# A gated S5 layer on one Trainium2 core: earlier norms and statistics, B in four transposes, and tanh gates until the phase tables are done

## The chip, the core and the metric

The kernel runs on one core of a Trainium2 chip. The metric is device time in microseconds (us) of one execution; the profile of an execution shows a span that is about 1.8 us shorter than its time. Executions are told apart by the mean clock that TensorE was granted: the kernel before has executions near 220.5 us at a clock of 0.975 and executions near 225.3 us at 0.953. The record calls an execution slow when it is over 1.5% above the fastest of its kernel in the call, and ratios use fast executions alone.

The engines are TensorE (PE, matmuls), VectorE (DVE), ScalarE (ACT) and GpSimd (POOL).

## The reference, cut to what matters

The input is 2048 tokens of width 448 in bfloat16. A layer norm feeds two branches, whose product is added to the input:

```python
def reference(A_x, ...):
    x = A_x
    xn = _layernorm(x)                       # mean and variance over the 448 columns
    # branch A, S5: a complex diagonal recurrence over the tokens
    #   Bu = xn @ B_bar ; h[t] = Lam_bar * h[t-1] + Bu[t] ; y = 2*Re(h @ C) + xn*Dskip
    s = _A_ref(xn, ...)
    # branch B: (sigmoid(xn @ w_gate) * (xn @ w_up)) @ w_down, inner width 1792
    g = _silu(_B_ref(xn, ...))
    return x + s * g
```

## The kernel before

The tokens go in 4 chunks of 512 (4 tiles of 128 tokens each). For each chunk TensorE computes 14 gate units (`gu`: a gate and an up product, 1.62 us a unit), 4 B units (`bu`), 4 down products (2.65 us each) and 4 y products (1.51 us each). ScalarE takes the gate and B results out of PSUM, the memory that matmuls write to (an eviction); VectorE multiplies, runs the scan and finishes y. A plan, made when the program is built, lays the engines' instructions in order: `side` is a queue of VectorE work put between matmul units, `add_late` defers work until a planned time, `force` plays the queues forward until a condition holds.

The row statistics are per chunk. Two VectorE instructions a tile give mean and variance; a chain of about 20 operations on 128x4 elements then makes the row scale `rsd` (a reciprocal square root, by three Newton steps for every chunk but chunk 0). In the kernel before, chunk 0's chain is on VectorE, the others' on GpSimd:

```python
def stat_chain(g, t0, n):
    G = V if g == 0 else nc.gpsimd
    ...                                        # cut: cast, + eps, negated mean
    for _ in range(3):
        G.tensor_tensor(out=q, in0=y, in1=y, op=ALU.mult)
        G.tensor_tensor(out=q, in0=q, in1=ve, op=ALU.mult)
        G.tensor_scalar(out=q, in0=q, scalar1=-0.5, scalar2=1.5, op0=ALU.mult, op1=ALU.add)
        G.tensor_tensor(out=y, in0=q, in1=y, op=ALU.mult)
    G.tensor_tensor(out=sd_b, in0=y, in1=ve, op=ALU.mult)

    def fin():
        V.reciprocal(out=rsd[:, ts, :], in_=sd_b)
        rs_done.add(g)
    plan.add_late(plan.dve + T_CHAIN, 0.15, fin)
```

The statistics come late, and the norms stand at fixed places, whether their chain is done or not (`force` puts the reciprocal in front):

```python
for pt in range(4):
    side += [... nu_1 .. nu_4 of pt ...]       # cut: sine and cosine tables of the recurrence
side.append((0.0, emit_edges))
side.append((0.9, emit_neg))
side.append((2.2, emit_coeffs))
for i in range(4):
    side.append((0.7, lambda i=i: stat(2, 8, i, 4)))
side.append((0.0, lambda: stat_chain(2, 8, 4)))
...                                            # chunk 3's statistics: inside the scan of chunk 0

def norm_slot(tt, on_vector):
    ...                                        # cut
    xm = norm_a(tt, False)                     # ScalarE
    plan.force(lambda: tt // CT in rs_done)
    norm_b(tt, xm, False)                      # ScalarE, needs rsd
    dup(tt)                                    # GpSimd copy of 64 columns
    dma_transpose(tt)                          # xn -> xnT, which feeds the matmuls
...
run_phase(G(0, 2, 8) + mixed(G(0, 8, 14), Bs(0), 2), [], spread(norms(1, True), 4, 5) + [(3, b_fix)])
run_phase(u, spread(downs(0), 1, 8), spread(norms(2), 2, 8))
run_phase(u, spread(ys(0), 2, 4) + spread(downs(1), 3, 8), spread(norms(3), 1, 7))
```

B arrives in 8 transposing transfers, and one GpSimd copy (`b_fix`, into `bT`) moves a part to its place; in GpSimd's order it stands behind chunk 1's chain. The first 16 gate units use tanh and the others use sigmoid; tanh is in the same ScalarE table as the sine here (in the traces no table load stands between them), so that tables are loaded 4 times in all.

Of the kernel before, what the change touches and what calls it, by code (L numbers as in the profile page):

```python
# [36 lines left out]
N_TANH = FT + 2  # L37
# [72 lines left out]
def kernel(  # L110
# [26 lines left out]
    plan = Plan()  # L137

# [5 lines left out]
    warm = w.tile([P, 512], BF16, name="warm")  # L144
    nc.gpsimd.memset(warm[:], 0.0)
# [16 lines left out]
    bT = w.tile([P, 4, 7 * P], BF16, name="bT")  # L162
    bw = w.tile([P, 1, 384], BF16, name="bw")
# [3 lines left out]
    vrow = w.tile([1, 3, 512], BF16, name="vrow")  # L167
# [11 lines left out]
    def load_b():  # L179
        for k, mat in enumerate((A_B_re, A_B_im)):  # L180
            a, b = 384 * k, 768 + H * k
            nc.sync.dma_start_transpose(out=bT[:, 0:3, a:a + 384], in_=mat[0:384, 0:384])
            if k == 0:
                nc.sync.dma_start_transpose(out=bw[:], in_=mat[0:384, 320:448])
            else:
                nc.sync.dma_start_transpose(out=bT[:, 3:4, a:a + 384], in_=mat[0:384, 320:448])
            nc.sync.dma_start_transpose(out=bT[:, 0:3, b:b + H], in_=mat[384:448, 0:384])
            nc.sync.dma_start_transpose(out=bT[:, 3:4, b:b + H], in_=mat[384:448, 320:448])
# [12 lines left out]
    load_w(512, 1152)  # L201
    load_b()
    load_w(1152, F)
# [3 lines left out]
    load_x(8, 4)  # L207
    load_x(12, 4)
# [3 lines left out]
    def emit_warm(n):  # L212
        for _ in range(n):
            nc.tensor.matmul(wps[:, 0, :], lhsT=warm[:, 0:P], rhs=warm[:], start=True, stop=True)  # L214
# [4 lines left out]
    T_CHAIN = 9.0  # L219
# [11 lines left out]
    def stat_chain(g, t0, n):  # L231

        G = V if g == 0 else nc.gpsimd
        mv = mvs[g]

        def t(name, dt=FP32):
            return w.tile([P, n, 1], dt, name=f"{name}{g}")[:]

        ts = slice(t0, t0 + n)
        var_b, ve_b, mean_b = t("var_b", BF16), t("ve_b", BF16), t("mean_b", BF16)  # L240
        G.tensor_copy(out=var_b, in_=mv[:, :, 1:2])
        G.tensor_single_scalar(out=ve_b, in_=var_b, scalar=EPS, op=ALU.add)
        if g == 0:
            sd_b = t("sd_b", BF16)
            nc.scalar.activation(sd_b, ve_b, ACT.Sqrt)
        G.tensor_copy(out=mean_b, in_=mv[:, :, 0:1])
        G.tensor_single_scalar(out=nmean[:, ts, :], in_=mean_b, scalar=-1.0, op=ALU.mult)
        if g == 0:
            V.reciprocal(out=rsd[:, ts, :], in_=sd_b)
            return  # L250
        ve, y, q, sd_b = t("ve"), t("y"), t("q"), t("sd_b", BF16)
        G.tensor_copy(out=ve, in_=ve_b)
        G.tensor_scalar(out=y.bitcast(I32), in0=ve.bitcast(I32), scalar1=-0.5, scalar2=RS_MAGIC,
                        op0=ALU.mult, op1=ALU.add)
# [8 lines that stand above are left out]
            V.reciprocal(out=rsd[:, ts, :], in_=sd_b)  # L263
            rs_done.add(g)

        plan.add_late(plan.dve + T_CHAIN, 0.15, fin)

# [27 lines left out]
    def pe_transpose(tt, eng):  # L295
        xn, xnT, j = xns[tt // CT][:, tt % CT, :], xnTs[tt // CT], tt % CT
        tp = ps.tile([P, 4, P], BF16, name="tpx", tag="acc", bufs=2)
        for kt in range(4):
            nc.tensor.transpose(tp[:, kt, :], xn[:, kt * P:(kt + 1) * P], ident[:, :])
        dst = xnT[:, :, j * P:(j + 1) * P]  # L300
# [36 lines left out]
    ones = cp.tile([P, NTAB], BF16, name="ones", tag="xnd_", bufs=1)  # L337

# [5 lines left out]
    def emit_columns():  # L344
# [9 lines left out]
        nc.scalar.activation(dt_b[:], vps[:, 0, :], ACT.Exp)  # L354
        K.update(vps=vps, vsb=vsb, dt_b=dt_b, lre=vsb[:, 1, :], lim=vsb[:, 2, :])

    def emit_decay():
        V.tensor_copy(out=K["vsb"][:], in_=K["vps"][:])
# [79 lines left out]
    def c_steps():  # L438
        cT = w.tile([P, 7, D], BF16, name="cT")
        K["cT"] = cT  # L440
        steps = []

        def step(dst, r, re, im, sa, sb):
            tmp = fp.tile([P, D], FP32, name="ctmp", tag="sig")
            nc.scalar.activation(tmp[r, :], re, ACT.Copy, scale=sa)
            V.scalar_tensor_tensor(out=dst, in0=im, scalar=sb, in1=tmp[r, :], op0=ALU.mult, op1=ALU.add)

        for m in range(7):
            def go(m=m):
                c2, n2i, n2r = K["c2"], K["n2i"], K["n2r"]  # L450
                if m < 6:
                    pt = m % 3
                    sa, sb = (c2, n2i) if m < 3 else (n2i, n2r)
                    step(cT[:, m, :], slice(0, P), crT[:, pt, :], ciT[:, pt, :], sa[:, pt:pt + 1], sb[:, pt:pt + 1])
                else:
                    hi = slice(H, P)
                    step(cT[0:H, 6, :], hi, cw[hi, 0, :], cw[hi, 1, :], c2[hi, 3:4], n2i[hi, 3:4])
                    step(cT[hi, 6, :], hi, cw[hi, 0, :], cw[hi, 1, :], n2i[hi, 3:4], n2r[hi, 3:4])
            steps.append((0.65 if m < 6 else 1.3, go))
        return steps  # L460
# [25 lines left out]
    LO, HI, ALL = slice(0, H), slice(H, P), slice(0, L)  # L486
    hFs = {}
    hF_done = set()
    n_gate = [0]
# [17 lines left out]
    def gu_act(c, ft):  # L507
# [3 lines left out]
        tanh = n_gate[0] < N_TANH  # L511
        n_gate[0] += 1
# [24 lines left out]

    def bu_unit(c, pt, half_first):
        bu = ps.tile([P, 2, 512], FP32, name="bu")
        if pt < 3:  # L540
            ms, halves = (pt, pt + 3), ((LO, bT[LO, 3, pt * P:(pt + 1) * P]), (HI, bT[HI, 3, 384 + pt * P:384 + (pt + 1) * P]))
        else:
            ms, halves = (6,), ((HI, bT[HI, 3, 768:896]),)
        unit_mms([bu[:, i, :] for i in range(len(ms))], ALL, xnTs[c],
                 [(lambda kt, m=m: bT[:, kt, m * P:(m + 1) * P]) for m in ms], halves, half_first)
# [110 lines left out]
    T_UNIT, T_ACT, T_DOWN, T_Y = 1.55, 1.3, 2.65, 1.55  # L656
# [38 lines left out]
    act(scr[:], pio2[:], ACT.Exp)  # L695
# [6 lines left out]
    for i in range(2):  # L702
        stat(0, 0, i, 4)
    emit_decay()
    for i in range(2, 4):
        stat(0, 0, i, 4)
    act(scr[:], pio2[:], ACT.Sqrt)
    stat_chain(0, 0, 4)
    nc.gpsimd.memset(ones[:], 1.0)
    for j in range(2):  # L710
        norm_b(j, norm_a(j, True), True)
        dup(j)
        pe_transpose(j, "v")
        emit_warm(1)
    xm = [norm_a(j, False) for j in (2, 3)]
    for j in (2, 3):
        norm_b(j, xm[j - 2], False)
        dup(j)
    act(scr[:], pio2[:], ACT.Silu)
    A, B = slice(0, 256), slice(256, 512)  # L720
    for f in range(2):
        gu_mm(0, f, A, f == 1)
    for j in (2, 3):
        pe_transpose(j, "v")
    for f in range(2):
        gu_mm(0, f, B, f == 1)
    plan.pe = plan.dve = 0.0
    for f in range(2):
        cost, fin = gu_act(0, f)
        plan.add_late(1.2 + 1.1 * f, cost, fin)  # L730

    side = plan.side
    side.append((0.6, emit_theta))
    side.append((1.2, emit_iota))
    new_xn(1)
    new_xnT(1)
    for i in range(4):
        side.append((0.7, lambda i=i: stat(1, 4, i, 4)))
    side.append((0.0, lambda: stat_chain(1, 4, 4)))
# [3 lines left out]
    side.append((0.0, emit_edges))  # L743
    side.append((0.9, emit_neg))
    side.append((2.2, emit_coeffs))
    for i in range(4):
        side.append((0.7, lambda i=i: stat(2, 8, i, 4)))
    side.append((0.0, lambda: stat_chain(2, 8, 4)))

    def ssm(c):  # L750
        side.append((1.15, lambda: emit_xnd(c)))
        ss = ssm_steps(c)
        if c == 0:
            st3 = [(0.7, lambda i=i: stat(3, 12, i, 4)) for i in range(4)]
            st3.append((0.0, lambda: stat_chain(3, 12, 4)))
            extra = c_steps() + st3
# [10 lines left out]
    def norm_slot(tt, on_vector):  # L767
        if tt % CT == 0 and tt >= 8:
            new_xn(tt // CT)
            new_xnT(tt // CT)  # L770
        if on_vector:
            V_norm(tt)
            return
        xm = norm_a(tt, False)
        plan.force(lambda: tt // CT in rs_done)
# [4 lines left out]
    def V_norm(tt):  # L780
        def fin():
            plan.force(lambda: tt // CT in rs_done)
            norm_b(tt, norm_a(tt, True), True)
            dup(tt)
            dma_transpose(tt)
            xn_done.add(tt)
        plan.add_late(plan.pe, 0.8, fin)

    def run_phase(units, sides, extras):

        n = len(units) // 2
        for p in range(n):
# [5 lines left out]
            for q, fn in extras:  # L798
                if q == p:
                    fn()  # L800
# [26 lines left out]
    def norms(c, a=False):  # L827
        return [lambda i=i: norm_slot(c * CT + i, a) for i in range(CT)]

    def b_fix():  # L830
        nc.gpsimd.tensor_copy(out=bT[LO, 3, 0:384], in_=bw[HI, 0, :])

    run_phase(G(0, 2, 8) + mixed(G(0, 8, 14), Bs(0), 2), [], spread(norms(1, True), 4, 5) + [(3, b_fix)])
# [4 lines left out]
    run_phase(u, spread(downs(0), 1, 8), spread(norms(2), 2, 8))  # L838
    ssm(2)
    u = mixed(G(2, 0, 4), Bs(2)) + G(2, 4, 14)  # L840
    run_phase(u, spread(ys(0), 2, 4) + spread(downs(1), 3, 8), spread(norms(3), 1, 7))
# [34 lines left out]
```

## Time and profile before

| | before (first profile) |
|---|---|
| time, median of 3 | 224.98 us (220.81 to 225.73) |
| profiled execution | 225.65 us, span 223.9, clock 0.953: a slow one |
| TensorE busy | 199.6 us |
| VectorE busy | 178.2 us |
| ScalarE busy | 121.5 us |
| GpSimd busy | 33.4 us |

The page of the profile, its busy times, its rows for TensorE and TensorE's clock in 40 equal slices (tenths, 9 is full), and the shares of the chain that ended last:

```profile
span 223.9 us, 2849 instructions
...
PE 199.6 (89%) x978; PEld 83.6 (37%) x978; DVE 178.2 (80%) x379; ACT 121.5 (54%) x218; POOL 33.4 (15%) x88
...
PE   7689985989998399938999999999999999969993
...
PEclk9969996799999889995999999999999999999999
...
DVE 51%; PE 22%; POOL 12%; ACT 8%; issue 4%; DMA 1%; POOLq 0%; ACTq 0%
```

TensorE is the busiest, and it has three holes: slices 7, 14 and 18 (a slice is 5.6 us). Near each the clock row falls too. TensorE's timeline shows them. Its columns are start, length, engine, line, operation, out<-in, sizes and count; in brackets is the idle time before it, and what ended it:

```profile
36.31 0.60 PE L476 MATMUL bu<-xnT,bT 64*128 64x512 bf16 x2 [3.58 <-POOL bT L831]
...
37.27 1.46 PE L470 MATMUL gu<-xnT,wg 128*128 128x512 bf16 x3
...
76.23 0.39 PE L476 MATMUL bu<-xnT,bT 64*128 64x512 bf16 x2 [4.29 <-ACT bus_857 L548]
76.56 2.74 PE L470 MATMUL bu<-xnT,bT 128*128 128x512 bf16 x6
...
101.71 1.46 PE L470 MATMUL gu<-xnT,wg 128*128 128x512 bf16 x3 [4.42 <-DMA xnT<-xn]
```

Each idle ends with a different releaser. After the first and the third, three matmuls of a gate take 1.46 us, where elsewhere in the same trace three take 0.81 us: half the clock, 0.43 us a matmul instead of 0.216. After the second, six matmuls of B take 2.74 us, where six took 1.46 at 31.27 us. The Trainium skill, "TensorE: Matmul & The Clock Gate", section "What's actually happening", says that the clock falls to half after one idle window of about 3.4 us; these three idles, of 3.58 to 4.42 us, agree with it.

What lies behind them shows on GpSimd and ScalarE. GpSimd's timeline, the first and the last operation of chunk 1's chain, and the copy behind it:

```profile
26.17 0.68 POOL L241 CAST var_b_418<-mv_362 128x4 bf16<-128x4 f32 x1 [15.04 <-DVE mv_362 L226]
...
35.49 0.20 POOL L260 TENSOR_TENSOR sd_b_428<-y_426,ve_425 128x4 bf16<-128x4 f32 x1
35.75 0.50 POOL L831 COPY bT<-bw 64x384 bf16<-64x384 bf16 x1
```

ScalarE's timeline, before the second hole:

```profile
73.64 0.67 ACT L289 ACTIVATE xn<-xm,rsd 128x448 bf16<-128x448 bf16 x1 [5.36 <-DVE rsd L263]
...
75.16 1.02 ACT L548 CAST bus_857<-bu 128x1024 bf16<-128x1024 f32 x1
```

GpSimd's timeline, before the third hole, the copy for the last tile of chunk 2:

```profile
98.99 0.23 POOL L293 COPY xn<-xn 128x64 bf16<-128x64 bf16 x1
```

The chain on GpSimd took 9.5 us, and the copy of B that TensorE needs came only after it. For chunk 2 a norm on ScalarE waited 5.36 us for the row scale, and the eviction that TensorE needs stood behind that norm. The copy at 98.99 us stood behind chunk 3's chain, which was on GpSimd until 99.04, and the transpose of the third hole came after the copy.

### The profile page before, as it was taken

The numbers are of one execution on the slowest core, as the hardware profiler recorded it, in microseconds if no ns is written. First come the engines' busy times: TensorE is split into PE (matmuls) and PEld (weight loads), VectorE is DVE, ScalarE is ACT, GpSimd is POOL, SyncE is SP. The second block draws the span as 40 slices with busy tenths as digits, with TensorE's granted clock in tenths as the row PEclk, the third lists the DMA queues.
The fourth block names the chain that finished last, engine by engine and source line by source line (L and its number), as shares of the span: only waits on it lengthen the run. The fifth ranks groups of instructions, "written<-read, shape, count | busy, mean of one in ns | idle before, by whom it ended". The sixth has DMA issues, their size and how long they took to land.

```text
span 223.9 us, 2849 instructions
## 1 busy us (share of the span) xinstructions
PE 199.6 (89%) x978; PEld 83.6 (37%) x978; DVE 178.2 (80%) x379; ACT 121.5 (54%) x218; POOL 33.4 (15%) x88
## 2 busy tenths in 40 slices
PE   7689985989998399938999999999999999969993
PEld 2254331323433133412344444434434444425551
DVE  5736993481998179996669999999999999999943
ACT  2816673578782898731574657656443555501310
POOL 5100284010068101860000000000000000000000
PEclk9969996799999889995999999999999999999999
DMA  5995799230000111000032010100000000001001
GB/s 125 297 211 85 237 313 214 81 74 3 0 1 0 23 26 23 0 11 14 0 26 65 21 44 1 26 0 0 21 22 23 21 0 0 3 21 63 0 21 62
DMA packets 23268, 12.19 MB, mean 54 GB/s; under 512 B 14643, under 2 KB 23222, under 8 KB 23254
## 3 DMA queue, kind: packets, MB, share of 16 engines
q1 hardware_dynamic: 23200, 11.90, 21.5%
q0 software_dynamic: 48, 0.11, 0.6%
q8 instruction: 7, 0.11, 0.2%
q14 instruction: 7, 0.06, 0.1%
q10 hardware_dynamic: 6, 0.00, 0.0%
HBM read 6.77 MB, written 1.84 MB: 38 GB/s over the span
## 4 chain that ended last, share of the span: by engine, by line
DVE 51%; PE 22%; POOL 12%; ACT 8%; issue 4%; DMA 1%; POOLq 0%; ACTq 0%
DVE wv L584 9%; PE gu L470 8%; PE acc L665 5%; DVE stats L225 3%; DVE hT L604 3%; PE acc L680 3%; DVE g_t L686 3%; DVE tb L565 2%; DVE ta L565 2%; DVE hFa L526 2%; DVE z L578 2%; DVE hFb L526 2%; PE bu L470 2%; DVE x_all L687 2%; PE wps L214 2%
## 5 line engine op out<-in xcount | busy, mean ns | idle before, releaser
L470 PE MATMUL gu<-xnT,wg 128*128 128x512 bf16 (+1 forms) x174 | 48.9, 393 | 6.0 <-DMA xnT<-xn 4.4
L470 PE MATMUL gu<-xnT,wu 128*128 128x512 bf16 (+1 forms) x174 | 48.5, 390 | 0.0
L519 ACT ACTIVATE sig<-gu 128x512 bf16<-128x512 f32 x40 | 23.9, 597 | 30.2 <-PE gu L476 22.8
L470 PEld LDWEIGHTS <-wg 128*128 128x128 bf16 x174 | 15.6, 101 | 31.3 <-issue 14.6
L470 PEld LDWEIGHTS <-wu 128*128 128x128 bf16 x174 | 17.8, 102 | 21.1 <-issue 2.8
L668 ACT ACTIVATE sigd<-acc 128x448 bf16<-128x448 f32 x16 | 8.7, 541 | 30.3 <-PE acc L665 30.3
L665 PE MATMUL acc<-wd,hFb 128*128 128x448 bf16 x112 | 23.8, 353 | 0.0
L665 PE MATMUL acc<-wd,hFa 128*128 128x448 bf16 x112 | 23.8, 353 | 0.0
L680 PE MATMUL acc<-cT,hT 128*128 128x448 bf16 x112 | 23.8, 352 | 0.0
L520 ACT CAST ub<-gu 128x512 bf16<-128x512 f32 x40 | 23.2, 581 | 0.0
L470 PE MATMUL bu<-xnT,bT 128*128 128x512 bf16 x84 | 23.1, 412 | 0.0
L476 PE MATMUL gu<-xnT,wk 64*128 64x512 bf16 (+1 forms) x116 | 19.0, 388 | 0.0
L515 ACT ACTIVATE th<-gu 128x512 f32<-128x512 f32 x16 | 9.5, 596 | 12.6 <-PE gu L476 9.5
L680 PEld LDWEIGHTS <-hT 128*128 128x128 bf16 x112 | 11.0, 98 | 13.0 <-issue 2.8
L665 PEld LDWEIGHTS <-hFa 128*128 128x128 bf16 x112 | 11.0, 98 | 10.7
L665 PEld LDWEIGHTS <-hFb 128*128 128x128 bf16 x112 | 11.0, 98 | 10.2
L476 PE MATMUL bu<-xnT,bT 64*128 64x512 bf16 x28 | 6.6, 411 | 9.0 <-ACT bus_857 L548 4.3
L293 POOL COPY xn<-xn 128x64 bf16<-128x64 bf16 x16 | 4.4, 282 | 67.4 <-ACT xn L289 52.5
L526 DVE TENSOR_TENSOR hFa<-sig,ub 128x512 bf16<-128x512 bf16 x19 | 7.9, 417 | 7.2 <-ACT ub L520 7.1
L470 PEld LDWEIGHTS <-bT 128*128 128x128 bf16 x84 | 7.5, 103 | 15.3 <-issue 7.9
L686 DVE TENSOR_TENSOR g_t<-acc,g_t 128x448 bf16<-128x448 f32 x16 | 9.9, 618 | 1.9 <-PE acc L680 1.8
L524 DVE SCALAR_TENSOR_TENSOR hFb<-th,ub 128x512 bf16<-128x512 f32 x7 | 4.8, 690 | 7.7 <-ACT ub L516 7.7
(271 smaller groups left out, 298.1 us busy)
## 6 DMA issues: line engine op xcount, KB each, us to landing
out_dram<-x_all SPq DMA_DIRECT2D x16, 112.0 KB, 1.7
wd<-in_B_w_down_dram SPq DMA_DIRECT2D x1, 1568.0 KB
x_all<-in_A_x_dram SPq DMA_DIRECT2D x3, 448.0 KB, 6.1
wg<-in_B_w_gate_dram SPq DMA_DIRECT2D x2, 480.0 KB, 3.8
wu<-in_B_w_up_dram SPq DMA_DIRECT2D x2, 480.0 KB, 6.9
x_all<-in_A_x_dram SPq DMA_DIRECT2D x2, 224.0 KB, 2.8
wg<-in_B_w_gate_dram SPq DMA_DIRECT2D x1, 384.0 KB, 7.8
wu<-in_B_w_up_dram SPq DMA_DIRECT2D x1, 384.0 KB, 8.4
```

Source lines behind the costliest of these rows:

```text
L470: nc.tensor.matmul(banks[i][:, cols], lhsT=fulls[i](kt), rhs=xnT[:, kt, cols], start=(kt == 0 and not half_first), stop=(kt == KF - 1 and ...
L476: nc.tensor.matmul(banks[i][:, cols], lhsT=ap, rhs=xnT[r, 3, cols], start=half_first, stop=not half_first)
L515: nc.scalar.activation(th[:], gu[:, 0, :], ACT.Tanh, scale=0.5)
L519: nc.scalar.activation(th[:], gu[:, 0, :], ACT.Sigmoid)
L520: nc.scalar.copy(out=ub[:], in_=gu[:, 1, :])
L526: V.tensor_tensor(out=hF, in0=th[:], in1=ub[:], op=ALU.mult)
L565: V.tensor_tensor(out=t[dst][:], in0=src, in1=tab, op=ALU.mult)
L584: V.tensor_tensor_scan(out=t["wv"][:, k, :], data0=rb, data1=t["z"][:, k, :], initial=(st[pt][:, k, :] if c else 0.0), op0=ALU.mult, op1=A ...
L665: nc.tensor.matmul(dacc[:, 0:D], lhsT=hF_at(c, ft)[:, j * P:(j + 1) * P], rhs=wd[:, ft, :], start=(ft == 0), stop=(ft == FT - 1))
L668: nc.scalar.activation(sigd[:], dacc[:, 0:D], ACT.Sigmoid)
L680: nc.tensor.matmul(y[:, 0:D], lhsT=hTs[c][:, hm, j * P:(j + 1) * P], rhs=K["cT"][:, cm, :], start=False, stop=(i == 6))
L686: V.tensor_tensor(out=g_t[:], in0=y[:, 0:D], in1=g_t[:], op=ALU.mult)
```

## The change

Its intent has four parts: take chunk 1's statistics off GpSimd, and so free its norms and the copy of B; take the statistics of chunks 2 and 3 early, and put their norms into ScalarE's order only when their chain is planned to be done; fetch B in fewer transfers; keep tanh until the tables are built, whatever the count, so that no sine falls between sigmoids. The prologue is reordered as well: the first table load is that of the square root, and the decay's work goes behind the first norms. The core of the diff:

```diff
-        G = V if g == 0 else nc.gpsimd
+        G = nc.gpsimd if g > 1 else V
...
-        plan.add_late(plan.dve + T_CHAIN, 0.15, fin)
+        if G is V:
+            fin()
+        else:
+            plan.add_late(plan.dve + T_CHAIN, 0.15, fin)
... (B: 4 transposes, with two more GpSimd copies)
-                nc.sync.dma_start_transpose(out=bT[:, 0:3, a:a + 384], in_=mat[0:384, 0:384])
... (7 more lines out)
+            nc.sync.dma_start_transpose(out=bT[:, 0:3, cols], in_=mat[:, 0:384])
+            nc.sync.dma_start_transpose(out=bT[:, 3:4, cols], in_=mat[:, 320:448])
... (gates)
-        tanh = n_gate[0] < N_TANH
-        n_gate[0] += 1
+        tanh = "cosL" not in K
... (plan constants)
-    T_UNIT, T_ACT, T_DOWN, T_Y = 1.55, 1.3, 2.65, 1.55
+    T_UNIT, T_ACT, T_DOWN, T_Y = 1.62, 2.8, 2.65, 1.55
... (order of the side work)
+    for i in range(1, 4):
+        side.append((0.7, lambda i=i: stat(1, 4, i, 4)))
+    side.append((1.2, emit_iota))
+    side.append((3.0, lambda: stat_chain(1, 4, 4)))
     side.append((0.6, emit_theta))
+    for i in range(4):
+        side.append((0.7, lambda i=i: V_norm(4 + i)))
+    side.append((1.15, lambda: emit_xnd(0)))
+    for i in range(4):
+        side.append((0.7, lambda i=i: stat(2, 8, i, 4)))
+    side.append((0.0, lambda: stat_chain(2, 8, 4)))
... (tables of phase 0, emit_edges, then stat of chunk 3, emit_neg, emit_coeffs, stat_chain of chunk 3)
... (norms of chunks 2 and 3: only with a finished chain)
+            while extras and extras[0][0] <= p and (p == n - 1 or not extras[0][2] or extras[0][2]()):
+                extras.pop(0)[1]()
...
+        return [(s_, fn, lambda: c in rs_done and c - 2 in xnds)
+                for s_, fn in spread([lambda i=i: norm_slot(c * CT + i) for i in range(CT)], lo, hi)]
```

Left out: the prologue's lines, the C matrices' steps (each ScalarE half issued two steps ahead of its VectorE half), and the transposed copy of chunk 0's last columns.

## The prediction

> **What bounds it now.** The page gives TensorE 199.6 us busy of 223.9, VectorE 178.2, ScalarE 121.5, GpSimd 33.4. From 119 to 198 us the table of windows shows TensorE busy 100% and VectorE 98%: balanced.. From the first full gate (18.3 us) TensorE's needed work, at its warm durations, is 54 gate units x 1.62 + 4 x 5.8 (B) + 16 x 2.65 (down) + 16 x 1.51 (y) = 177 us; it takes 202, so about 24 are stalls, seen in TensorE's timeline:
> - 31-43 us: 3.6 us idle on the GpSimd copy into bT, which stands behind chunk 1's statistics chain on GpSimd (26.2-35.7), then a half clock (12 matmuls in 5.2 us, 0.43 us each instead of 0.216): together 6.9.
> - 71.9-80: 4.3 idle on a ScalarE B eviction, itself behind the xn ACTIVATE that waited 5.4 us for the GpSimd chain of chunk 2; plus half clock: 6.0.
> - 97.3-107: 4.4 idle on the xnT transpose; tile 11's GpSimd copy stood behind chunk 3's chain (89.2-99): 7.1 with half clock.
> - 3.8 in small gaps near 50-55 and 198-202.
>
> The half clock agrees with the Trainium skill, "TensorE: Matmul & The Clock Gate", "What's actually happening" (an idle window of about 3.4 us halves the clock): each idle above 3.5 us is followed by 0.43 us matmuls.
>
> **What the change does.**
> - Chunk 1's chain goes to VectorE: +20 small operations, estimate 3.0 us (the 21 coefficient operations took 3.1). The B copies no longer stand behind it: -6.9 on TensorE.
> - Statistics of chunks 2 and 3 and their GpSimd chains (10 us each) are issued early, norms only once finished; nothing waits for them: -13.
> - Tanh gates last until the tables are done: 18 instead of 16, +0.25 us each (0.60 against 0.33). No sine falls after the first sigmoid, so no extra table load (1.28 us).
> - Prologue: first table load is Sqrt, decay moves behind the norms: row scale at about 7.3 instead of 8.2 us, xn of tile 1 at 8.7 instead of 10.5, fewer cold matmuls; but the first weights land near 10-11.5. Gain 1 to 3.5 us.
> - B in 4 instead of 8 transposes (1.2-1.9 us issue each), but behind the last weights: expected by 26-28 us, first use near 29: stall of 0-3 us possible. The transposes of chunk 1 queue behind those of C: landing near 39-42, need near 41.
>
> **Sum.** First full gate near 16; +177 +3.9 tail +1.75 (run time over span) = 199 without stalls. VectorE: about 182 us in all, 172 of them after 16 us, so also near 197: both engines nearly full. I add 6 us for lags: 205 us, range 199 to 212; chances: faster 0.95, within 2% 0.04, slower 0.01.
>
> **What would show it.** VectorE busy about 182 us; TensorE busy down to about 190 with under 10 us of idle after 18 us; no GpSimd copy or ScalarE xn wait above 3 us before TensorE; no idle above 3.4 us between 18 and 190 us; granted clock near full in 30-110 us; chunk 1 gates starting near 42, chunk 2's near 82 (before 101.7); the chain of waits shifting to VectorE.
>
> **What would make it wrong.** B or chunk 1's xnT landing late, with a half clock after it; VectorE lagging so that y of chunk 0 or the last hF's hold TensorE; slow executions (before: 220.8 to 225.7); the prologue bound by weights.

## The result, and the profile after

The change came to 208.44 us (median of 4; 207.82 to 208.46 for the three fast executions), against 223.16 for the kernel before. The ratio of fast runs is 0.9392, with a 95% interval of 0.9311 to 0.9473. A ratio here is the record's, made from mean times of fast runs, so it isn't quite the ratio of the medians quoted; from the means of the fast runs listed (208.24, and 221.08 for 220.81 and 221.35) it would be 0.942, inside that interval.

The fourth execution took 284.18 us, and it was the one profiled. Its page, the span and TensorE's clock row:

```profile
span 282.4 us, 2836 instructions
...
PEclk9666666666666666666666666666666666666666
```

The clock is at 0.66 from the second slice to the end, not in holes. Nothing of that is used for the change: the same kernel was run again, five times, at 207.8 to 208.43 us and a clock near 0.99 (experiment e1 below), and the profile after is from there. The page of the change, in the same lines as before:

```profile
span 206.0 us, 2851 instructions
...
PE 193.0 (94%) x984; PEld 82.3 (40%) x984; DVE 181.7 (88%) x398; ACT 121.2 (59%) x217; POOL 24.6 (12%) x66
...
PE   7999999699999969999999999999999999589992
...
PEclk9999999999999999999999999999999999969999
...
DVE 56%; PE 25%; ACT 14%; issue 2%; DMA 1%; ACTq 0%
```

The three holes in the TensorE row are gone, and so is the GpSimd share of the chain (it was 12%). What is left are shallow dips in slices 8 and 15, and one at slice 35, the only one with a fall of the clock behind it. TensorE's timeline of the change, the three largest idles after the first full gate and the matmuls behind the last:

```profile
41.02 0.37 PE L475 MATMUL bu<-xnT,bS 64*128 64x512 bf16 x1 [1.59 <-ACT bus L551]
...
75.68 0.81 PE L469 MATMUL gu<-xnT,wg 128*128 128x512 bf16 x3 [2.05 <-ACT ub L516]
...
180.77 0.35 PE L681 MATMUL acc<-xnd,ident 128*128 128x448 bf16 x1 [2.58 <-DVE g_t L689]
180.96 2.33 PE L683 MATMUL acc<-cT,hT 128*128 128x448 bf16 x7
...
196.29 1.49 PE L683 MATMUL acc<-cT,hT 128*128 128x448 bf16 x7
```

After 2.05 us of idle the clock stayed full (0.81 us for three); after 2.58 us it fell to half: seven matmuls took 2.33 us, where the same seven took 1.49 us later. The windows of the change give each engine's busy time by stage. The columns are the window, its length, busy us (and count) of TensorE, weight loads, VectorE, ScalarE and GpSimd, then TensorE's clock, the DMA share and GB/s:

```profile
15.00:42.00 27.00, 25.39 (x125) 9.36 (x125) 25.55 (x69) 18.56 (x32) 10.80 (x23) 1.00 0.96 206
42.00:76.00 34.00, 30.89 (x153) 12.51 (x152) 26.61 (x69) 32.67 (x61) 10.41 (x27) 1.00 0.07 14
76.00:120.00 44.00, 44.00 (x224) 18.58 (x222) 43.07 (x86) 27.97 (x50) 1.08 (x4) 1.00 0.10 25
178.00:206.00 28.00, 21.75 (x105) 10.47 (x103) 19.04 (x37) 3.87 (x8) 0.00 (x0) 0.93 0.10 33
```

From 42 to 76 us the full engine is ScalarE, with 32.67 of 34 us, though its share of the whole span is 59%. From 76 on TensorE is never idle until 178. The copies that B needs are on GpSimd, early:

```profile
22.54 0.73 POOL L833 COPY bT<-bT 64x448 bf16<-64x448 bf16 x1 [18.85 <-DMA bT<-in_A_B_re_dram]
...
24.33 0.54 POOL L835 COPY bS<-bT 128x256 bf16<-128x256 bf16 x1 [0.26 <-DMA bT<-in_A_B_im_dram]
```

They are over at 24.87 us; the first B matmul is at 27.95 and doesn't wait.

### The profile page after: what moved, and what is told of

It is laid out like the page before. It is cut to its first block, busy times and chain, and to the rows that moved or that the text cites. A ratio compares the mean times of both kernels' runs of the same rounds, so it can differ in the third digit from the quotient of the medians.

```text
span 282.4 us, 2836 instructions
## 1 busy us (share of the span) xinstructions
PE 274.0 (97%) x969; PEld 98.8 (35%) x984; DVE 186.5 (66%) x398; ACT 122.9 (44%) x217; POOL 18.4 (7%) x66
## 4 chain that ended last, share of the span: by engine, by line
PE 97%; issue 1%; DVE 0%; ACT 0%; POOL 0%; POOLq 0%
PE gu L469 39%; PE acc L668 23%; PE acc L683 11%; PE bu L469 10%; PE gu L475 7%; PE wps L208 3%; PE bu L475 2%; PE acc L681 2%; PE tpx L296 0%; ACT bus_624 L551 0%; PE tpx L298 0%; DVE g_t L689 0%; POOL ones L145 0%; PE vps L347 0%; DVE x_all L690 0%
## 5 line engine op out<-in xcount | busy, mean ns | idle before, releaser
L469 PE MATMUL gu<-xnT,wu 128*128 128x512 bf16 (+1 forms) x171 | 65.0, 504 | 0.4
L469 PE MATMUL gu<-xnT,wg 128*128 128x512 bf16 (+1 forms) x164 | 61.3, 488 | 1.4 <-issue 0.6
L668 PE MATMUL acc<-wd,hFa 128*128 128x448 bf16 x112 | 35.3, 476 | 0.1
L683 PE MATMUL acc<-cT,hT 128*128 128x448 bf16 x112 | 34.9, 472 | 0.0
L668 PE MATMUL acc<-wd,hFb 128*128 128x448 bf16 x112 | 34.4, 468 | 0.0
L475 PE MATMUL gu<-xnT,wk 64*128 64x512 bf16 (+1 forms) x116 | 22.8, 455 | 0.2 <-issue 0.2
L511 ACT ACTIVATE th<-gu 128x512 f32<-128x512 f32 x18 | 10.7, 596 | 19.2 <-PE gu L475 10.1
L522 DVE TENSOR_TENSOR hFb<-sig,ub 128x512 bf16<-128x512 bf16 x21 | 8.9, 422 | 11.3 <-ACT ub L516 11.3
L676 DVE TENSOR_TENSOR g_t<-g_t,sigd 128x448 bf16<-128x448 bf16 x16 | 6.2, 387 | 11.4 <-ACT g_t L673 11.4
L520 DVE SCALAR_TENSOR_TENSOR hFa<-th,ub 128x512 bf16<-128x512 f32 x11 | 7.5, 687 | 7.5 <-ACT ub L512 7.5
L475 PEld LDWEIGHTS <-wk 64*128 64x128 bf16 x116 | 3.9, 94 | 21.8 <-issue 21.7
```

Source lines behind the costliest of these rows:

```text
L469: nc.tensor.matmul(banks[i][:, cols], lhsT=fulls[i](kt), rhs=xnT[:, kt, cols], start=(kt == 0 and not half_first), stop=(kt == KF - 1 and ...
L475: nc.tensor.matmul(banks[i][:, cols], lhsT=ap, rhs=xnT[r, 3, cols], start=half_first, stop=not half_first)
L511: nc.scalar.activation(th[:], gu[:, 0, :], ACT.Tanh, scale=0.5)
L520: V.scalar_tensor_tensor(out=hF, in0=th[:], scalar=1.0, in1=ub[:], op0=ALU.add, op1=ALU.mult)
L522: V.tensor_tensor(out=hF, in0=th[:], in1=ub[:], op=ALU.mult)
L668: nc.tensor.matmul(dacc[:, 0:D], lhsT=hF_at(c, ft)[:, j * P:(j + 1) * P], rhs=wd[:, ft, :], start=(ft == 0), stop=(ft == FT - 1))
```

## The experiments

Twelve kernels ran, four on a chip. All gave a correct result. "Before" is the kernel before, run in the same rounds. The change in e1's call is what the others are measured against; for e6 to e12 that is a comparison across chips. The record's rule at 2% calls the change faster and leaves every ratio of this table unclear, so small differences go by the intervals.

| run | what it is | median us | ratio to before (95%) |
|---|---|---|---|
| e1 | the change, unaltered | 208.02 | 0.9425 (0.9398 to 0.9452) |
| e2 | before + chunk 1's chain on VectorE | 218.11 | 0.9884 (0.9826 to 0.9941) |
| e3 | before + early statistics and guarded norms | 220.47 | 0.9885 (0.9793 to 0.9977) |
| e4 | e2 and e3 together | 211.86 | 0.9601 (0.9547 to 0.9656) |
| e5 | before, unaltered, one run | 219.13 | none |
| e6 | change, chunk 1's chain on GpSimd | 206.58 | 0.9336 (0.9234 to 0.9438) |
| e7 | change, late statistics | 208.44 | 0.9413 (0.929 to 0.9535) |
| e8 | change, tanh for 16 gates | 216.24 | 0.9774 (0.9631 to 0.9917) |
| e9 | change, late statistics and no guard | 213.76 | 0.9685 (0.9581 to 0.9789) |
| e10 | change, old prologue | 209.85 | 0.9498 (0.9432 to 0.9563) |
| e11 | change, y of chunk 2 in other PSUM banks | 204.85 | 0.9273 (0.9172 to 0.9374) |
| e12 | e6, e11 and chunk 2's norms on VectorE | 203.91 | 0.9242 (0.9168 to 0.9316) |

For e3 the median includes two slow executions; its fast ones were 219.47 and 216.9. The executions of e8 fall into two pairs, 214.7 at a clock of 0.98 and 217.7 at 0.968.

### e1: the change again

No edit. Expected:

> The changed kernel unaltered, because its first profile fell into a throttled execution (clock 0.66). Theory A (three waits on GpSimd chains and the half clock behind them are what the change removes): ratio 0.935 to 0.945 again; TensorE busy near 190 us and idle under 10 us after 18 us, no idle above 3.4 us after 18 us, clock near 1 in 30-110 us. Rival R (both engines are full, so VectorE takes back part of what the waits gave): the same ratio, but TensorE idle of over 8 us in many pieces, released by VectorE.

Measured: 208.02 us, five executions within 0.63 us. The 284 us execution is not a property of the kernel that shows again. This run gives the profile after, shown above.

### e2, e3, e4: the two halves, alone and together

Three kernels, each from the kernel before. e2 moves chunk 1's chain alone:

```diff
-        G = V if g == 0 else nc.gpsimd
+        G = V if g <= 1 else nc.gpsimd
-        plan.add_late(plan.dve + T_CHAIN, 0.15, fin)
+        if G is V:
+            fin()
+        else:
+            plan.add_late(plan.dve + T_CHAIN, 0.15, fin)
```

> The kernel before with one part alone: chunk 1's statistics chain on VectorE (about 3 us more VectorE work), same issue order otherwise. Theory A: the copy into bT starts as soon as B has landed, the 3.6 us idle near 31 us and the half clock behind it vanish or shrink to under 1 us: minus 5 to 7 us, ratio 0.97 to 0.98. Rival R: VectorE's 3 us and its lag take it back: ratio above 0.99. Rival B (B itself lands late, near 31 us or after, and the chain only seemed to hold the copy): the copy still starts after 31 us and the stall stays.

e3 takes the statistics of chunks 2 and 3 early and lets their norms wait for the chain:

```diff
-    T_CHAIN = 9.0
+    T_CHAIN = 12.0
...
     side.append((0.0, emit_edges))
+    for i in range(4):
+        side.append((0.7, lambda i=i: stat(2, 8, i, 4)))
+    side.append((0.0, lambda: stat_chain(2, 8, 4)))
     side.append((0.9, emit_neg))
     side.append((2.2, emit_coeffs))
     for i in range(4):
-        side.append((0.7, lambda i=i: stat(2, 8, i, 4)))
-    side.append((0.0, lambda: stat_chain(2, 8, 4)))
+        side.append((0.7, lambda i=i: stat(3, 12, i, 4)))
+    side.append((0.0, lambda: stat_chain(3, 12, 4)))
... (stat of chunk 3 out of the scan of chunk 0; the guard on the norms as in the change)
```

> The kernel before with another part alone: row statistics and GpSimd chains of chunks 2 and 3 issued in phase 0, right after the table edges, and their norms only once the chain is done; chunk 1's chain stays on GpSimd. Theory A: the idles of 4.3 us near 72 us and of 4.4 us near 97 us vanish with their half clock: minus 11 to 13 us, ratio 0.94 to 0.95; the stall near 31 us stays. Rival R: VectorE, which used those idles to catch up, now holds TensorE elsewhere: minus 2 to 6 us, ratio 0.97 to 0.99.

e4 is both edits in one kernel.

> Both parts together on the kernel before; what is left to the full change is the prologue, B in 4 transposes, the longer tanh stretch and the plan's constants. Theory A: the gains add, minus 16 to 20 us, ratio 0.91 to 0.93 less what VectorE's lag costs; so near or a little above the full change, 0.94 to 0.95, with the prologue's 1 to 3.5 us missing. Rival R: not more than the better of the two parts plus 2 us.

Measured: 1.2% each alone, 4.0% together, so together they gave more than the sum of the two. None met its Theory A: 5 to 7 us were expected of e2, 11 to 13 of e3 and 16 to 20 of e4, and about 2.6, 2.6 and 8.8 were measured. In e2 the first hole went, and the second shrank to 2.75 us (with half clock behind it), but the third stayed (4.53 us at 94.74, on xnT). In e3, whose profile is of a slow execution, the first hole stayed (3.58 us at 35.85); the other two went, but smaller ones came in their place, of 1.96 and 2.46 us. TensorE's timeline of e3, at the first of these:

```profile
53.38 1.44 PE L470 MATMUL gu<-xnT,wg 128*128 128x512 bf16 x3 [1.96 <-DMA xnT<-xn]
```

Three matmuls at half clock, after an idle of only 1.96 us, which followed another of 1.10 us three microseconds earlier. In e4 three idles of 1 us or more are left: 1.11, 2.46 and 3.00 us. What follows: with one hole filled, waits are left or come up elsewhere, and a small wait can still bring half clock with it. Savings of such holes can't be taken one by one and added. With e4 at 211.86, and the change at 208.02 on the same chip, about 3.8 us of the change's gain are from neither half; the prologue is about half of that (e10).

### e5: the kernel before, looked at in a fast execution

No edit. Expected:

> The kernel before unaltered, for a profile of a fast execution (the first one fell into a slow one of 225.65 us). Time 220 to 221.5; the same three idles of 3.6, 4.3 and 4.4 us on the GpSimd copy, the B eviction and the xnT transpose; the fast state should differ by one of the half-clock stretches missing (granted clock 0.975 against 0.953, which is worth 0.5 x (0.047 - 0.025) x 2 x 220 = 4.8 us).

Measured: 219.13 us at a clock of 0.984. By its time and clock it belongs with the fast ones. TensorE's timeline of e5, at the same three places as the slow execution that the prediction was read from:

```profile
34.10 0.39 PE L476 MATMUL bu<-xnT,bT 64*128 64x512 bf16 x2 [1.43 <-POOL bT L831]
...
71.09 0.39 PE L476 MATMUL bu<-xnT,bT 64*128 64x512 bf16 x2 [4.29 <-ACT bus L548]
...
96.57 1.46 PE L470 MATMUL gu<-xnT,wg 128*128 128x512 bf16 x3 [4.42 <-DMA xnT<-xn]
```

The second and third hole are the same to the hundredth. The first is another: 1.43 us on the copy of B, not 3.58, and no half clock after it (0.93 us more were idle at 29.20, on a transfer of weights). Its first full gate stands at 16.78 us, not at 18.34. So the 6.9 us that the prediction put on the first hole were a reading of a slow execution. This agrees with e2, where filling that hole was worth 1.2%, or 2.6 us of 221.

### e6: chunk 1's chain on GpSimd, but at its early place

```diff
-        G = nc.gpsimd if g > 1 else V
+        G = nc.gpsimd if g > 0 else V
...
-        if G is V:
-            fin()
+        if g == 1:
+            K["fin1"] = fin
...
-    side.append((3.0, lambda: stat_chain(1, 4, 4)))
+    side.append((0.0, lambda: stat_chain(1, 4, 4)))
     side.append((0.6, emit_theta))
+    side += [(0.45, lambda: nu_1(0)), (0.43, lambda: nu_2(0)), (0.65, lambda: nu_3(0)), (0.43, lambda: nu_4(0))]
+    side.append((0.15, lambda: K["fin1"]()))
...
-    for pt in range(4):
+    for pt in range(1, 4):
```

> The changed kernel with chunk 1's chain on GpSimd again, but everything else at the place the change gives it (statistics from 12.4 us, so the chain can run from about 15.5 to 25 and the B copies to about 27.5, first use at 27.95). Theory A1 (it is the place in time that counts, not the engine): within 1% of the changed kernel, ratio to before 0.94 to 0.95, B product of chunk 0 delayed by less than 1.5 us. Rival A2 (the engine counts: a GpSimd chain ahead of the B copies stalls TensorE as before): idle above 3 us at the first B product with half clock behind it, 5 us or more, ratio 0.96 to 0.97.

Measured: 206.58 us (206.38 to 206.92). That is about 1.4 us less than the change, across two calls, so its size isn't settled to better than their spread. That the move to VectorE isn't needed is settled. What the gain needed is the early place: in e6 chunk 1's chain still stands ahead of the copies of B on GpSimd, but it is over at 24.50 us and the copies at 27.99, and the first B matmul, at 28.44, doesn't wait.

The move even had a price, which shows on ScalarE. ScalarE's timeline of the change, its last cosine and the table load after it:

```profile
51.07 0.34 ACT L398 ACTIVATE cth<-v,pio 128x4 f32<-128x4 f32 x1
...
52.69 1.28 ACT L671 ACT_TABLE_LOAD   x1
```

The same of e6:

```profile
47.45 0.31 ACT L398 ACTIVATE cth<-v,pio 128x4 f32<-128x4 f32 x1
47.78 1.28 ACT L515 ACT_TABLE_LOAD   x1
```

Without the chain on VectorE (3.5 us in the change, from 18.56 to 22.05), and with the first table's work put into the time that GpSimd takes for it, the tables are done 3.6 us sooner, and ScalarE is free of them earlier in its crowded stretch. The two parts of this edit were not run apart. The windows of e6 for that stretch:

```profile
42.00:76.00 34.00, 33.18 (x162) 13.43 (x164) 29.75 (x76) 32.61 (x61) 10.19 (x28) 1.00 0.08 17
```

ScalarE is as full as in the change (32.61 against 32.67 us), but TensorE does 33.18 us of work instead of 30.89. Of the 2.3 us only 1.4 reach the end. An idle of 1.04 us on VectorE comes up at 150.23, where the change had none, and the idle near 180 us is 2.88 instead of 2.58.

### e7 and e9: early statistics, and the guard on the norms

e7 puts the statistics of chunks 2 and 3 back to their late places, but leaves the norms waiting for their chain:

```diff
-    for i in range(4):
-        side.append((0.7, lambda i=i: stat(2, 8, i, 4)))
-    side.append((0.0, lambda: stat_chain(2, 8, 4)))
... (and stat of chunk 3 with its chain)
     side.append((3.0, emit_coeffs))
-    side.append((0.0, lambda: stat_chain(3, 12, 4)))
+    for i in range(4):
+        side.append((0.7, lambda i=i: stat(2, 8, i, 4)))
+    side.append((0.0, lambda: stat_chain(2, 8, 4)))
...
+            extra = extra[2:] + [(0.7, lambda i=i: stat(3, 12, i, 4)) for i in range(4)]
+            extra.append((0.0, lambda: stat_chain(3, 12, 4)))
```

> The changed kernel with the row statistics of chunk 2 behind the coefficients and those of chunk 3 inside the scan of chunk 0, where the kernel before has them; norms still only once the chain is done. Theory A: chunk 3's chain again stands on GpSimd ahead of the last copies of chunk 2, xnT of chunk 2 comes late: an idle of 2 to 5 us before chunk 2's first gates, 3 to 7 us in all, ratio to before 0.955 to 0.975. Rival G (only the rule that norms wait for their chain matters, not the early statistics): within 1 us of the changed kernel, 0.94 to 0.947.

Measured: 208.44 us (206.44 to 209.53), within 0.5 us of the change. By the number the rival was right: as long as no norm stands in ScalarE's order before its row scale is there, the statistics may come late. But the trace shows a gain and a loss in that number. With these statistics no longer ahead of them, the tables are done at 48.10 us instead of 51.41, as in e6, where that came with a gain. In return the row scale of chunk 2 is there only at 67.81 us, and its four norms then fill ScalarE from 69.35 to 74.50 us, ahead of the evictions of gates. TensorE's timeline of e7:

```profile
76.38 1.44 PE L469 MATMUL gu<-xnT,wg 128*128 128x512 bf16 x3 [2.98 <-ACT ub L516]
```

That idle is longer than the 2.05 us of the change, and half clock follows it. So e7 shows that the guard is enough to keep the long holes away; it doesn't show that early statistics are worth nothing.

e9 takes the guard away too, so the norms stand at the fixed places of the kernel before:

```diff
... (all of e7)
+        xm = norm_a(tt, False)
         plan.force(lambda: tt // CT in rs_done)
-        xm = norm_a(tt, False)
...
-        return [(s_, fn, lambda: c in rs_done and c - 2 in xnds)
+        return [(s_, fn, None)
-    run_phase(u, spread(downs(0), 1, 8), norms(2, 1, 6))
+    run_phase(u, spread(downs(0), 1, 8), norms(2, 2, 8))
-    run_phase(u, spread(ys(0), 2, 4) + spread(downs(1), 3, 8), norms(3, 1, 6))
+    run_phase(u, spread(ys(0), 2, 4) + spread(downs(1), 3, 8), norms(3, 1, 7))
```

> The changed kernel with late statistics of chunks 2 and 3 AND norms at fixed places again (issued whether or not their chain is done, as in the kernel before); the late statistics alone cost nothing. Theory N (the gain of the middle is that no norm is issued on ScalarE ahead of its chain, and no copy behind a chain; either the early statistics or the rule is enough): both long idles come back, a ScalarE wait for the row scale of over 3 us and an xnT wait before chunk 2's gates, 6 to 10 us more, ratio to before 0.97 to 0.985. Rival M (with the rest of the change in place the waits no longer reach TensorE): less than 2 us more, 0.94 to 0.95.

Measured: 213.76 us, 5.7 more than the change. The profiled execution is the slowest of four, 215.53 us; the others took 212.78 to 213.99. ScalarE's timeline of e9:

```profile
67.97 0.67 ACT L286 ACTIVATE xn<-xm,rsd 128x448 bf16<-128x448 bf16 x1 [3.04 <-DVE rsd L257]
```

And TensorE's timeline of e9, a little later:

```profile
70.56 0.61 PE L475 MATMUL bu<-xnT,bT 64*128 64x512 bf16 x2 [7.63 <-ACT bus L551]
71.11 2.74 PE L469 MATMUL bu<-xnT,bT 128*128 128x512 bf16 x6
```

The mechanism of the second hole is back: the norm waits on ScalarE for the row scale, the eviction of B stands behind it, TensorE is idle for 7.63 us and goes on at half clock (six matmuls in 2.74 us, as after the second hole before). Of the 7.63 us only 3.04 are ScalarE's wait for the row scale; just before it ScalarE was on steps of the C matrices, which waited for VectorE too.

The third hole came back only as a wait of 0.44 us, but its mechanism is there: the last copy of chunk 2 starts at 89.95 us, behind chunk 3's chain (over at 90.01), its transpose follows, and the gates of chunk 2 wait for it until 92.78 us. TensorE came there late, at 92.34 us, after the hole before, so the one hole hides the other. In the surroundings of the change, statistics and guard together are thus worth 5.7 us, not the 13 that the prediction counted for these two holes. With late statistics that is the guard (e7 against e9, which also moves the norms' slots a little). Early statistics with the norms at fixed places were not run; in the change chunk 2's chain ends at 43.34 us, long before the norm that waits in e9.

### e8: tanh for the first 16 gates, as before

```diff
-        tanh = "cosL" not in K
+        n_gate[0] += 1
+        tanh = n_gate[0] <= FT + 2
```

> The changed kernel with the old rule: 16 tanh gates, then sigmoid, so two sigmoid gates come before the last sine tables and ScalarE loads its tables 4 times more (8 loads instead of 4, 1.28 us each: 5.1 us). Theory S (since the change ScalarE bounds 42 to 76 us, where it is busy 97%): 3 to 5 us more, ratio to before 0.955 to 0.965. Rival (ScalarE has slack there, TensorE and VectorE bound): less than 1 us, 0.94 to 0.947.

Measured: 216.24 us, 8.2 more than the change and 7.8 more than e7. This median lies between two pairs of executions, which are 6.7 and 9.7 above the change. The expected price, four more table loads of 1.28 us, is 5.1, and 3 to 5 was the forecast of Theory S. ScalarE's timeline of e8, around the first of them:

```profile
47.45 0.74 ACT L389 ACTIVATE cosT<-v,pio 128x512 bf16<-128x512 f32 x1
48.21 1.28 ACT L517 ACT_TABLE_LOAD   x1
49.50 0.60 ACT L517 ACTIVATE sig<-gu 128x512 bf16<-128x512 f32 x1
...
50.59 1.28 ACT L383 ACT_TABLE_LOAD   x1
...
53.15 1.28 ACT L517 ACT_TABLE_LOAD   x1
...
55.53 1.28 ACT L395 ACT_TABLE_LOAD   x1
```

A sigmoid falls between two tables' sines, and each crossing loads a table. They fall into the stretch where ScalarE is full, and TensorE pays more than their sum. TensorE's timeline of e8:

```profile
63.00 0.61 PE L475 MATMUL bu<-xnT,bT 64*128 64x512 bf16 x2 [5.66 <-ACT bus L553]
```

An idle of 5.66 us, and half clock behind it. The rule for tanh adds nothing to what the kernel before had, which loaded 4 tables too. It is what makes the rest of the change possible: with norms and statistics ahead of them the tables end later, and a fixed count of 16 would be wrong.

### e10: the old prologue

```diff
-    act(scr[:], pio2[:], ACT.Sqrt)
+    act(scr[:], pio2[:], ACT.Exp)
...
-    for i in range(4):
+    for i in range(2):
+        stat(0, 0, i, 4)
+    V.tensor_copy(out=K["vsb"][:], in_=K["vps"][:])
+    emit_decay()
+    for i in range(2, 4):
         stat(0, 0, i, 4)
+    act(scr[:], pio2[:], ACT.Sqrt)
... (norms and transposes of chunk 0 in the old order, both first gate halves before the last transposes)
```

> The changed kernel with the old start: Exp tables first, decay between the statistics, tiles 2 and 3 normed after tiles 0 and 1, both first half gates ahead of the last two transposes, one warm matmul behind each transpose. Theory P: the first full gate starts near 16.8 us (clock kept) or 18.3 us (half clock in 9 to 16 us) instead of 15.0, and the delay reaches the end whole: 1.8 to 3.3 us more, in two groups, ratio to before 0.950 to 0.960. Rival: ScalarE bounds 42 to 76 us whatever the start, and the delay is absorbed: less than 0.8 us, 0.94 to 0.946.

Measured: 209.85 us, 1.8 more than the change. The first full gate moves from 15.02 to 17.03 us, and the rest of the trace is shifted by about those 2.0 us. Nothing downstream takes it up: what the prologue loses, the kernel loses. The size is good to less than a microsecond: in the seven traces with the change's prologue the first full gate stands at 15.02 to 15.85 us.

### e11: the end, two y tiles of chunk 2 in other PSUM banks

The idle of 2.58 us near 180 us waits for VectorE to finish with a PSUM buffer of the kind `acc`, of which there are two. The gate's buffers are free by then:

```diff
-        y = acc_tile()
+        if c == 2 and j > 1:
+            y = ps.tile([P, 2, 512], FP32, name="gu", bufs=2)[:, 0, :]
+        else:
+            y = acc_tile()
```

> The changed kernel with one thing more: at the end the last two y tiles of chunk 2 take the gates' PSUM banks, which are free by then, so TensorE doesn't wait for VectorE to clear the accumulator (2.6 us idle near 178 us, then 15 matmuls at half clock, 2 us). Theory T: the idle and half clock vanish, minus 2.5 to 4.5 us, ratio to before 0.922 to 0.932. Rival V (VectorE is what is late there, and the last y needs its last scan anyway): TensorE waits later instead, minus 0 to 1 us, 0.936 to 0.943.

Measured: 204.85 us, 3.2 less than the change. TensorE's timeline of e11, at that place:

```profile
178.72 0.35 PE L684 MATMUL gu<-xnd,ident 128*128 128x448 bf16 x1
178.91 1.49 PE L686 MATMUL gu<-cT,hT 128*128 128x448 bf16 x7
```

No idle, and full clock. The idle and its half clock had cost 2.58 + 1.7 = 4.3 us. That not all of it shows is in part a difference between the two profiled executions that has nothing to do with the edit: e11's has the idle of 2.05 us at 76.37 where e1's has it at 75.68, and it is that late from its first full gate on (15.70 us against 15.02).

### e12: what the runs pointed to, together

e6 and e11, and chunk 2's norms on VectorE instead of ScalarE:

```diff
+        if tt // CT == 2:
+            V_norm(tt)
+            return
```

> Chunk 1's chain on GpSimd as in the run that beat the change by 1.4 us, the tail as in the other kernel of this call, and the norms of chunk 2 on VectorE (0.6 us a tile there against 1.3 on ScalarE), which takes 5.4 us off ScalarE where it is 96% busy and adds 2.6 to VectorE. Theory: minus 1.4, minus 2.5 to 4.5, minus 0 to 2: 200.5 to 204 us, ratio to before 0.908 to 0.925. Rival V: VectorE is the bound from 76 us on, what it is given it gives back: 205 to 207 us, 0.93 to 0.936.

Measured: 203.91 us (203.26 to 205.6, 6 runs). This beats the kernel before by 7.6% and is 4.1 us under the change. The windows of e12 for the stretch in which ScalarE was full:

```profile
42.00:76.00 34.00, 33.57 (x168) 13.59 (x167) 30.52 (x81) 28.23 (x53) 7.30 (x28) 1.00 0.08 16
```

ScalarE went from 32.67 to 28.23 us there, and TensorE from 30.89 to 33.57 of 34. But e6, with ScalarE still full, had 33.18, so most of this is e6's edit, and taking four norms off ScalarE brought TensorE at most 0.4 us more in this stretch. The end shows 0.9 us against e11, with overlapping ranges: less than e6's edit gave alone. TensorE's timeline of e12 tells where it went back:

```profile
151.43 0.35 PE L668 MATMUL acc<-wd,hFa 128*128 128x448 bf16 x1 [2.25 <-DVE g_t L692]
```

An idle of 2.25 us, on VectorE, where the change had none and e6 had one of 1.04. That agrees with Rival V in kind: time won earlier seems to have become a wait for VectorE. No run has e6's and e11's edits without the norms, so whether the norms gain or lose stays open.

### What could not be tried

The change with the old constants of the plan (`T_UNIT` 1.55, `T_ACT` 1.3) deadlocks when it is built, so the share of those constants in the gain stays open. So does that of B's four transposes: in e4, which has the eight of before, the first B unit is at 30.18 us and doesn't wait either, but no run changed the transposes alone. The new steps of the C matrices were not run apart either. What was measured, 2.6 us (e2, from the kernel before), 5.7 (e9) and 1.8 (e10), makes 10.1 of the 12.7 us gained, but in different surroundings, so that the three don't strictly add.

## Why the prediction was right

The central value was 205 us and the change took 208.0 to 208.4, within the range given. Point by point:

1. *The sum upwards held.* It was 16 for the first full gate, 177 of TensorE work, 3.9 of tail, 1.75 of time over span and 6 of lags. The profiled execution of e1 took 207.8 us; its first full gate was at 15.02, so 207.8 - 15.0 - 177 - 3.9 - 1.8 = 10.1 us were lost between, not 6. That the total was only 3 us too low is in part luck: the start, 1 us earlier than predicted, hid a part of the 4.1. The busy time of TensorE, predicted at about 190, was 193.0; that of VectorE, 182, was 181.7; the idle of TensorE after 18 us, under 10, was 7.3.

2. *The mis-sized term is "I add 6 us for lags".* The prediction put it on two nearly full engines, TensorE and VectorE. Of the 10.1 us, 4.7 were idles that ScalarE ended (1.59, 0.34, 0.28, 0.44 and 2.05 us), 2.58 an idle that VectorE ended, and 1.7 the half clock after that: 16 matmuls, the first still at full clock, in 4.74 us, which take 3.02 at the full clock. About 1 us is left unassigned. The sum has no term for ScalarE, to which the page gave 54% of the span; the windows of the change show 32.67 of 34 us from 42 to 76. e8 shows that more work there costs more than its length. e6 points to what made the stretch tight: the sine and cosine work of the tables, which in the change ends 3.6 us later than in e6; in e6 the four idles after 42 us (0.34, 0.28, 0.44 and 2.05) are three of 0.21 to 0.23. That it is this work alone isn't shown: e6 also takes work off VectorE, and in e7, where the tables end as early, an idle of 2.98 us is left behind the norms. The VectorE part was foreseen in kind, and e11 shows it.

3. *The deductions were too large, and did no harm.* "-6.9 on TensorE" for the first hole was read from a slow execution: e5 shows 1.43 us and no half clock there in a fast one, and e2 found 2.6 us. "Nothing waits for them: -13" for the other two was measured as 5.7 us in the surroundings of the change (e9), where the one hole hides most of the other. They did no harm, since the time wasn't got by subtracting. From 225, less 6.9, 13 and 1 to 3.5 for the prologue, subtracting would have given 201.6 to 204.1, and from a fast execution of before, near 220.7, even 197.3 to 199.8. From that fast execution the change in fact gained 12.7 us.

4. *The mechanism of the holes was right; the ranking of the parts wasn't.* The GpSimd chain did stand before the copy of B, and the norm did stand before the eviction. But the first doesn't need VectorE (e6): the early place is enough. The other two don't need the early statistics (e7): the guard is enough. Whether early statistics without the guard would be enough too wasn't run.

5. *Tanh* was costed at two gates of 0.25 us. The order was foreseen rightly (18 tanh gates, 4 table loads), but not what hung on it: 6.7 to 9.7 us (e8).

6. *Prologue*: a gain of 1 to 3.5 us was predicted, and e10 shows 1.8. *B*: "expected by 26-28 us" came at 24.87, without a stall. *Chunks*: the gates of chunk 1 started at 41.98 (predicted 42), those of chunk 2 at 84.79 (predicted 82; 101.7 before).

7. *"The chain of waits shifting to VectorE"* was only half right: its share went from 51% to 56%, and ScalarE's from 8% to 14%.

## What to carry to other kernels

Build a predicted time upwards, from the work of the fullest engine and the moment at which it can start, and don't subtract stalls from the old time: here three stalls read as 20 us, and the whole change gained 12.7, because one was read from a slow execution and they don't add. Before trusting a share of the whole span, take busy times by stage: an engine at 59% of the span was busy for 32.67 of 34 us, and 3.1 of the 7.3 us of idle that were left lay there. When an engine that works in order has a wait in it, ask first whether the waiting instruction can stand later, before moving work to a faster engine.

## What the Trainium skill lacked or had wrong

- "TensorE: Matmul & The Clock Gate", section "What's actually happening": an idle of about 3.4 us as what halves the clock is too lenient a limit to plan by. Half clock also followed single idles of 2.46 us (e4), 2.58 us (the change), 2.98 us (e7), and 1.96 us in e3 with another of 1.10 shortly before; 2.05 us in the change and 2.25 us in e12 were not followed by it. The page does say that the window runs freely, and that the number of slow matmuls at the start of a kernel varies from run to run for that; these numbers fit a window that runs freely, and no run here shows the window itself.
- The same page, section "Seeing it yourself", knows a limiter at 13/16 of the clock when three cores of a die are busy, and says that one or two busy cores never trip it. Here one of 9 executions of the unaltered change, a program on one core, had a mean clock of 0.661 over the whole run, and took 284.18 us in place of 208. No page has a state of about two thirds of the clock that lasts for a whole run. What the other cores of the chip did then is not on record.
- "ScalarE: Activation LUTs", section "What ACT_TABLE_LOAD costs": the load of 1283 ns agrees with the trace (1.28 us). The further 1380 ns of drain for each switch do not show: in e8 the activation before the load ended at 48.19 us, the load started at 48.21, and the next activation started at 49.50, 0.01 us after the load ended.
- "GPSIMD Engine Reference", section "1. Specifications", says that GpSimd shares its SBUF interfaces with VectorE. Other pages of the skill have the rule of who then waits; what none gives is a time for operations of 128x4 elements beside a busy VectorE. In the change a product of 128x4 elements took 0.20 us on GpSimd while VectorE was idle, and 0.99 us some microseconds later while VectorE was in a scan, in GpSimd's timeline below (the profiler's spans on GpSimd are rough). Chunk 1's chain took 3.5 us on VectorE in the change, and 9.5 on GpSimd in the kernel before.

```profile
60.06 0.20 POOL L251 TENSOR_TENSOR q<-q,ve 128x4 f32<-128x4 f32 x1
...
64.13 0.99 POOL L251 TENSOR_TENSOR q<-q,ve 128x4 f32<-128x4 f32 x1
```
